# A pre-norm block (dilated local attention, then a squared-ReLU MLP) on one core: an order laid out by hand is replaced by a list scheduler, with MLP groups of four tiles, four-query attention items, and later tiles transposed by DRAM and VectorE

## Chip, cores, metric

One core of one Trainium2 chip. The metric is the device time of one execution in microseconds (us). The kernel before takes 528.69 us, the median of three runs (528.32 to 528.77).

## The reference

The input x is 2048 rows of 512 fp32 values. Both halves are residual:

```python
S, D, H, Dh, W, dil, F = 2048, 512, 32, 16, 8, 2, 1792
q, k, v = layernorm(x) @ wqkv           # 32 heads of 16
idx     = s - 2 * arange(8)             # each query sees 8 keys, two rows apart; masked below 0
o       = softmax(q . k[idx] / 4) @ v[idx]
h       = x + o @ wo
out     = h + relu(layernorm(h) @ w1 + b1) ** 2 @ w2 + b2
```

Work is in fp32 precision. TensorE multiplies fp32r operands, so each fp32 operand is split into a rounded part (names ending in h) and the rest (names ending in l), and a product is three passes: h by h, l by h, h by l.

## The kernel before

**Tiles.** The 2048 rows make 16 tiles of 128 rows. Rows are dealt so that a partition holds neighbouring queries of one parity: four tiles form a unit in which each partition has four queries (R = 4) that share a sliding window of keys, and a half-unit of two tiles (RI = 2) is called s.

**Stages.** (1) Projections: for each tile x is loaded, normalised, transposed on PE (`transposes`, L156: four 128x128 transposes into a PSUM tile `tr`), rounded by ACT (`hi`, L116) and subtracted by DVE (`lo`, L119). Then `qkv` multiplies it with the split wqkv in four pieces of 384 columns (`mm3`, L178). ACT copies the result out (L422) and SP stores it to a DRAM array `qkv_d` (L408). (2) Attention, on DVE, runs beside the projections and the MLP: an item is a half-unit by a quarter of the heads. Its windows of k and v and its q come back from `qkv_d` (L197, L210), ACT copies q to PSUM (`qp`, L217). DVE multiplies q with the eight shifted views of the window (L273) and reduces over the head's 16 values, takes a softmax, and multiplies with v (L284). Each long DVE operation has 1024 elements per partition. POOL sums over the eight keys in three halving steps (`add_up`, L343). (3) Output product: o is transposed on PE, split, and multiplied with wo (`wo_product`). DVE adds x, giving h. (4) h is normalised, transposed on PE and split, then `mlp1` and `mlp2` (L560) go over F in 14 steps of 128. A group of two tiles has 256 columns in the first product, and there are six of them; the last four tiles form one wide group of 512 columns. All of w1 and w2 is split once and stays on chip; w2 takes the space of wqkv when the projections are done.

**What sets the order.** Each engine runs its instructions in program order, and the program is written out by hand. PE's sequence is cut into slots. `at(delta, ...)` puts a chore into a later slot, `after` behind the attention of that slot, and `end_slot(pe)` adds the slot's PE time to a clock. `pump` then emits attention instructions until their estimated DVE time has caught up with that clock:

```python
while (done[until] < G) if until is not None else (now["dve"] < now["pe"]):
```

All large transfers are issued by SP, in one queue. `ready_next` places the next half-unit's loads, o transposes and output products among the steps of the current MLP group, and its h is transposed between the last three steps of that group (`h_T`).

Of the kernel before, what the change touches and what calls it, by code (L numbers as in the profile page):

```python
# [15 lines left out]
P = 128  # L16
KB = D // P
FB = F // P
R = 4
RI = 2  # L20
NS = S // P // RI
G = 8
GH = H // G
GC = GH * DH
CH = S // 2
PAD = W
EPS = 1e-5
NEG = -4.0e9
ROWS = 15
LAG = 3  # L30
SLOW = 1.1, 1.05
LAST = 2
LAGW = 2
DELAY = 3
WJ = 2
WARM = 18
# [3 lines left out]
def block_kernel(ctx, tc, x, wqkv, wo, w1, b1, w2, b2, out):  # L40
# [11 lines left out]


    CS = (CH + PAD) * GC
    qkv_d = dram.tile([2, G // 2, 3, 2, CH + PAD, GC], F32, name="qkv_d")

    def chain(e, g, c, r, ap):
        block = ((e * (G // 2) + g // 2) * 3 + c) * 2 + g % 2
        return bass.AP(tensor=qkv_d.tensor, offset=qkv_d.offset + block * CS + r * GC, ap=ap)

# [4 lines left out]

# [8 lines left out]
    wq_h = wpool.tile([P, KB, 3 * D], F32R, name="wq_h", tag="big_h")  # L74
    wq_l = wpool.tile([P, KB, 3 * D], F32R, name="wq_l", tag="big_l")
    wo_h = wpool.tile([P, KB, D], F32R, name="wo_h")
    wo_l = wpool.tile([P, KB, D], F32R, name="wo_l")
    w1_h = wpool.tile([P, KB, F], F32R, name="w1_h")
    w1_l = wpool.tile([P, KB, F], F32R, name="w1_l")
    w2_h, w2_l = {}, {}  # L80

    def row(name, shape=(P, D), dt=F32):
        return work.tile(list(shape), dt, name=name, tag="row", bufs=ROWS)

    due = {}
    late = {}
    now = {"slot": 0, "pe": 0.0, "dve": 0.0, "sub": 0}  # L90

    def at(delta, fn, *a):
        due.setdefault(now["slot"] + delta, []).append((fn, a))

    def after(delta, fn, *a):
        late.setdefault(now["slot"] + delta, []).append((fn, a))
# [8 lines left out]
    def run(chores):  # L105
        todo = chores.get(now["slot"], [])
        while todo:
            fn, a = todo.pop(0)
            fn(*a)

    def dve(t):
        now["dve"] += t


    def hi(dst, src):
        nc.scalar.copy(dst, src)  # L116

    def lo(eng, dst, src, h):
        eng.tensor_tensor(out=dst, in0=src, in1=h, op=ALU.subtract)  # L119

    stats = {}

    def norm_stats(key, src, delay=True):
        st = small.tile([P, 6], F32, name="st")
        mv = small.tile([P, 2], F32, name="mv", bufs=4)
# [13 lines left out]
        if delay:  # L139
            after(0, finish)  # L140
        else:
            finish()
# [662 lines left out]
```

## Time and profile before

| what | value |
|---|---|
| three runs | 528.69, 528.32, 528.77 us |
| profiled execution: span of its instructions | 527.5 us |
| busy share of the span: PE, PE weight load | 98%, 89% |
| DVE, ACT, POOL | 73%, 48%, 58% |
| DMA moved, all queues | 75.93 MB |
| SP's queue (q1), share of 16 engines | 75.26 MB, 47.6% |

The page gives one profiled execution, whose span lies 1.2 us below the median of the timed runs. A share of busy time is a mean over stages that differ: projections and attention run together up to about 215 us, then MLP groups and attention, and in the last 110 us almost only PE works. Instructions on PE overlap, so the time of one is read from the distance between starts.

### The profile page before, as it was taken

The numbers are of one execution on the slowest core, as the hardware profiler recorded it, in microseconds if no ns is written. First come the engines' busy times: TensorE is split into PE (matmuls) and PEld (weight loads), VectorE is DVE, ScalarE is ACT, GpSimd is POOL, SyncE is SP. The second block draws the span as 40 slices with busy tenths as digits, with TensorE's granted clock in tenths as the row PEclk, the third lists the DMA queues.
The fourth block names the chain that finished last, engine by engine and source line by source line (L and its number), as shares of the span: only waits on it lengthen the run. The fifth ranks groups of instructions, "written<-read, shape, count | busy, mean of one in ns | idle before, by whom it ended". The sixth has DMA issues, their size and how long they took to land.

```text
span 527.5 us, 8636 instructions
## 1 busy us (share of the span) xinstructions
PE 518.5 (98%) x3024; PEld 471.7 (89%) x3024; DVE 382.8 (73%) x571; ACT 252.0 (48%) x565; POOL 306.6 (58%) x421
## 2 busy tenths in 40 slices
PE   7899999999999999999999999999999999999997
PEld 6899999999999888988989898898989888888886
DVE  5559999998998799997998899699979323211113
ACT  4514554554347566545626464463536335442331
POOL 3514678788666479676877786876879717000000
PEclk8999999999999999999999999999999999999999
DMA  8578887898677453544544464454435000100002
GB/s 250 144 228 221 276 257 228 247 277 257 195 224 259 134 177 105 179 125 141 179 135 122 116 187 122 133 179 125 124 99 170 19 0 2 40 1 1 1 0 80
DMA packets 70803, 75.93 MB, mean 144 GB/s; under 512 B 6760, under 2 KB 47976, under 8 KB 70760
## 3 DMA queue, kind: packets, MB, share of 16 engines
q1 hardware_dynamic: 70616, 75.26, 47.6%
q8 instruction: 23, 0.38, 0.3%
q14 instruction: 20, 0.16, 0.1%
q10 hardware_dynamic: 144, 0.13, 0.1%
HBM read 58.50 MB, written 16.91 MB: 143 GB/s over the span
## 4 chain that ended last, share of the span: by engine, by line
PE 57%; issue 3%; POOL 3%; ACT 0%; DVE 0%; POOLq 0%; ACTq 0%
PE mm L178 25%; PE acc L560 25%; PE wo L178 5%; PE tr L156 2%; POOL rl L119 1%; POOL rs L135 1%; POOL h L497 0%; POOL pr L343 0%; PE half L581 0%; DVE pr L284 0%; POOL rs L137 0%; POOL rs L133 0%; ACT hn L151 0%; ACT r L537 0%; POOL o L343 0%
## 5 line engine op out<-in xcount | busy, mean ns | idle before, releaser
L343 POOL TENSOR_TENSOR pr<-pr 128x512 f32<-128x512 f32 (+1 forms) x128 | 131.5, 1027 | 36.8 <-DVE pr L284 31.5
L537 ACT ACTIVATE r<-mm,b_sb 128x256 f32<-128x256 f32 (+1 forms) x98 | 49.4, 505 | 120.0 <-PE mm L178 111.2
L119 POOL TENSOR_TENSOR rl<-r,rh 128x256 fp32r<-128x256 f32 x84 | 63.0, 754 | 57.6 <-ACT rh L116 57.5
L284 DVE TENSOR_TENSOR pr<-ex,v 128x1024 f32<-128x1024 f32 x64 | 78.0, 1220 | 5.5 <-POOL o L343 2.9
L273 DVE TENSOR_TENSOR pr<-qp,k 128x1024 f32<-128x1024 f32 x64 | 76.1, 1188 | 4.9 <-ACT qp L217 4.3
L178 PE MATMUL mm<-hh,w_h 128*128 128x256 f32 (+1 forms) x392 | 69.8, 300 | 0.0
L178 PE MATMUL mm<-hl,w_h 128*128 128x256 f32 (+1 forms) x392 | 69.0, 298 | 0.0
L178 PE MATMUL mm<-hh,w_l 128*128 128x256 f32 (+1 forms) x392 | 68.9, 298 | 0.0
L178 PEld LDWEIGHTS mm<-hh,w_h 128*128 128x128 f32 x392 | 59.9, 189 | 6.8 <-ACT r L537 0.2
L422 ACT COPY y<-mm 128x384 f32<-128x384 f32 x64 | 30.2, 480 | 65.3 <-PE mm L178 34.1
L560 PE MATMUL acc<-w_h,rh 128*128 128x512 f32 x192 | 58.8, 397 | 0.0
L178 PEld LDWEIGHTS mm<-hl,w_h 128*128 128x128 f32 x392 | 56.8, 191 | 2.2
L178 PEld LDWEIGHTS mm<-hh,w_l 128*128 128x128 f32 x392 | 56.7, 191 | 2.2
L560 PE MATMUL acc<-w_h,rl 128*128 128x512 f32 x192 | 57.8, 391 | 0.3 <-POOL rl L119 0.3
L560 PE MATMUL acc<-w_l,rh 128*128 128x512 f32 x192 | 57.9, 391 | 0.0
L178 PE MATMUL mm<-wq_h,xh 128*128 128x384 f32 x256 | 57.4, 344 | 0.1
L178 PE MATMUL mm<-wq_h,xl 128*128 128x384 f32 x256 | 55.6, 338 | 0.6 <-DVE xl L119 0.4
L178 PE MATMUL mm<-wq_l,xh 128*128 128x384 f32 x256 | 55.0, 335 | 0.0
L119 DVE TENSOR_TENSOR rl<-r,rh 128x512 fp32r<-128x512 f32 x14 | 9.7, 692 | 59.8 <-ACT rh L116 59.8
L178 PEld LDWEIGHTS mm<-wq_h,xl 128*128 128x128 f32 x256 | 45.9, 190 | 1.2 <-DVE xl L119 1.2
L178 PEld LDWEIGHTS mm<-wq_l,xh 128*128 128x128 f32 x256 | 45.7, 189 | 0.0
L538 ACT ACTIVATE r<-r 128x256 f32<-128x256 f32 (+1 forms) x98 | 44.0, 449 | 3.1
(84 smaller groups left out, 855.2 us busy)
## 6 DMA issues: line engine op xcount, KB each, us to landing
k<-qkv_d SPq DMA_DIRECT2D x48, 288.0 KB, 2.7
v<-qkv_d SPq DMA_DIRECT2D x48, 288.0 KB, 2.7
qkv_d<-y SPq DMA_DIRECT2D x32, 384.0 KB, 4.3
xt<-in_A_x_dram SPq DMA_DIRECT2D x16, 256.0 KB, 4.3
q<-qkv_d SPq DMA_DIRECT2D x32, 128.0 KB, 2.9
h<-in_A_x_dram SPq DMA_DIRECT2D x16, 256.0 KB, 3.8
out_dram<-h SPq DMA_DIRECT2D x15, 256.0 KB, 3.1
raw<-in_B_w_dram SPq DMA_DIRECT2D x16, 224.0 KB, 4.4
```

The source lines that it names most:

```text
L119: eng.tensor_tensor(out=dst, in0=src, in1=h, op=ALU.subtract)
L135: nc.gpsimd.tensor_tensor(out=rs[:, 0:1], in0=rs[:, 1:2], in1=mhalf, op=ALU.pow)
L156: nc.tensor.transpose(tr[:, k, :], src[:, k * P:(k + 1) * P], ident)
L178: nc.tensor.matmul(ps, l(k), r(k), start=(n == 0), stop=(n == 3 * KB - 1))
L273: nc.vector.tensor_tensor(out=pr.rearrange("p i w h d -> p i w (h d)"), in0=qp[:, j].unsqueeze(2).to_broadcast([P, RI, W, GC]), in1=kwin, ...
L284: nc.vector.tensor_tensor(out=p2, in1=vwin, op=ALU.mult, in0=e1[:, :, :, j * GH:(j + 1) * GH].unsqueeze(4).to_broadcast([P, RI, W, GH, DH]))
L343: nc.gpsimd.tensor_tensor(out=dst, in0=p2[:, :, :w], in1=p2[:, :, w:2 * w], op=ALU.add)
L422: nc.scalar.copy(y[:, :, t % RI * GC:(t % RI + 1) * GC], ps[:, :3 * GP].rearrange("p (j c) -> p j c", j=6))
L537: nc.scalar.activation(r, ps, AF.Relu, bias=b1_sb[:, f:f + 1])
L538: nc.scalar.activation(r, r, AF.Square)
L560: nc.tensor.matmul(acc[j], l[:, j * P:(j + 1) * P], w[f], start=(f == 0 and n < len(js)), stop=(f == last and n >= len(terms) - len(js)))
```

## The change

The source is rewritten; the arithmetic of the block stays the same.

- **Order.** Every piece of work becomes a task with engines that may run it, a guessed duration, and the tiles that it reads and writes. `deadlines` goes backward from PE's planned times, and `schedule` deals the tasks out, engine by engine, the one that can start first and is due first. The order that results is fixed before the program runs.
- **Transposes.** The first four x tiles and o and h of unit 0 are transposed on PE. All others (`turned`) go to DRAM in 512-byte pieces (`turn_write`), come back rearranged in 128-byte pieces (`turn_read`, 2048 a tile), and DVE transposes the 32x32 blocks (`turn`).
- **Projections.** The first four tiles as before; the other twelve in three products of 512 columns (q, k, v), stored two tiles at a time.
- **Attention.** An item is now four queries by 128 channels (a quarter of the heads); long DVE operations have 2048 elements. Logits and exponentials are in PSUM (`le`).
- **MLP.** Four groups of four tiles, all 512 columns wide. w1 has six of its 14 steps in space of its own and eight in wqkv's. w2 is split in the first group, written to DRAM (`w2_d`), and read again step by step in the other three, into four buffers (`w2s`).
- **Results.** h and the MLP results of units 0 to 2 are written to DRAM (`park_h`, `park`) and added at the end (`unpark`), together with b2.
- **Norms.** Statistics of x tiles 4 to 15 and of h of units 1 to 3 move from DVE to ACT (`norm_act`), those of the first tiles stay on DVE.

```diff
-G = 8
+Q = 32
+IQ = 2
+G = 4
+FA = 6
+BY_PE = (0,)
+TO_MLP = 10
...
+    def deadlines(self):
+        for t in reversed(self.tasks):
+            slack = SLACK[t.only] if t.only else 1.0
+            d = min([s.due for s in t.succs], default=1e6) - t.dur - t.lat - slack
+            if t.pe is not None:
+                d = t.pe
+            elif t.by is not None:
+                d = min(d, t.by)
...
+                    key = (s if s > free[eng] + 0.02 else free[eng],
+                           t.due - 1e3 if t.pe is not None and t.early else t.due, t.n)
+                    if pick is None or key < pick[0]:
+                        pick = key, t, s
+                if pick and (best is None or pick[2] < best[2]):
+                    best = eng, pick[1], pick[2]
...
-    def end_slot(pe):
-        now["pe"] += pe
-        run(due)
-        pump()
-        run(late)
-        now["slot"] += 1
...
+    def norm_act(src, dst):
+            nc.scalar.activation(sq.get(), src.get(), AF.Copy, accum_out=s[:, 0:1])
+            nc.scalar.activation(s[:, 1:2], s[:, 0:1], AF.Copy, scale=-1.0 / D)
+            nc.scalar.activation(sq.get(), src.get(), AF.Square, bias=s[:, 1:2],
+                                 accum_out=s[:, 2:3])
+            nc.scalar.activation(s[:, 3:4], s[:, 2:3], AF.Copy, scale=1.0 / D, bias=EPS)
...
+    def turn_write(d, src):
+        load(512, 512, lambda q: q.dma_start(
+            turn_ap(d, 0, [P, KB], [KB * D, Q], [D, KB], [1, P]),
+            src.get().rearrange("p (k m) -> p k m", k=KB)), r=[src], w=[("d", d)])
+    def turn_read(d, dst, n=1, r=()):
+        load(2048 * n, 128, lambda q: q.dma_start(
+            dst.get().rearrange("p (m c) -> p m c", c=Q),
+            turn_ap(d, 0, [Q, KB], [n * KB * D, Q], [P, n * KB * KB], [1, Q])),
+            r=list(r) + [("d", d)], w=[dst])
+    def turn(src, dst, part=slice(None)):
+        vec(D, lambda: nc.vector.transpose(dst.get().rearrange("p k m -> p (k m)"),
+                                           src.get()[:, part]), r=[src], w=[dst])
+    def turned(src):
+        d = Dram(dram.tile([P * D], F32, name="t_d"))
+        turn_write(d, src)
+        back, t = row("back"), row("turned", (P, KB, P))
+        turn_read(d, back)
+        turn(back, t)
+        return t
...
+    def item(u, g, due):
...
+        for n, i0 in enumerate((0, IQ)):
+            pr = buf("pr", (P, IQ, W, GC), name="pr")
+            vec(2048, lambda pr=pr, i0=i0: nc.vector.tensor_tensor(
+                out=pr.get(),
+                in0=qp.get()[:, i0:i0 + IQ].unsqueeze(2).to_broadcast([P, IQ, W, GC]),
+                in1=window(ks.get(), i0, [1, GC]), op=ALU.mult),
+                r=[qp, ks], w=[pr], by=due + 5 * n)
...
+    def w1_of(part, f):
+        if f < FA:
+            return w1a[part][:, f]
+        return big[part][:, KB + f - FA, :].rearrange("p (k c) -> p k c", k=KB)
...
+    def first_w2(f):
+        raw = row("raw2")
+        load(128, 2048, lambda q: q.dma_start(raw.get(), w2[f * P:(f + 1) * P, :]), w=[raw],
+             ahead=AHEAD)
+        t = buf("pair", (P, 2, D), F32R, "w2s")
+        hi(D, lambda: t.get()[:, 0], raw.get, r=[raw], w=[(t, 0)])
+        lo(D, lambda: t.get()[:, 1], raw.get, lambda: t.get()[:, 0], r=[raw, (t, 0)], w=[(t, 1)])
+        load(128, 4096, lambda q: q.dma_start(w2_d[f], t.get().bitcast(F32)), r=[(t, 0), (t, 1)],
+             w=[("w2d", f)], by=plan.pe + 5)
+        return t
+    def get_w2(f):
+        t = buf("pair", (P, 2, D), F32R, "w2s")
+        load(128, 4096, lambda q: q.dma_start(t.get().bitcast(F32), w2_d[f]), r=[("w2d", f)],
+             w=[(t, 0), (t, 1)], ahead=AHEAD)
+        return t
...
+    def park(t, a):
+        m = row("m")
+        plan.add({"ACT": ac(D), "DVE": dv(D)},
+                 lambda e: nc.scalar.copy(m.get(), a.get()) if e == "ACT"
+                 else nc.vector.tensor_copy(m.get(), a.get()), r=[a], w=[m], by=plan.pe)
+        load(128, 2048, lambda q: q.dma_start(m_d[t], m.get()), r=[m], w=[("md", t)],
+             by=plan.pe + 5)
+    def unpark(t, due):
+        m, h = row("m"), row("h")
+        load(128, 2048, lambda q: q.dma_start(m.get(), m_d[t]), r=[("md", t), "done"], w=[m],
+             by=due)
+        load(128, 2048, lambda q: q.dma_start(h.get(), h_d[t]), r=[("hd", t), "done"], w=[h],
+             by=due)
+        tt("DVE", D, m.get, m.get, lambda: b2_sb, ALU.add, r=["b2"], w=[m], by=due + 5)
+        tt("DVE", D, m.get, m.get, h.get, ALU.add, r=[h], w=[m], by=due + 5)
+        b, e, i = where(t)
+        load(128, 2048, lambda q: q.dma_start(out_v[b, e, i], m.get()), r=[m], by=due + 8)
...
-    def x_T(t):
-        tr = transposes(xt.pop(t))
-        xT[t] = row("xh", (P, KB, P), F32R), row("xl", (P, KB, P), F32R)
-        at(0, hi_T, tr, [xT[t][0]])
-        after(0, lo_T, tr, [xT[t][0]], [xT[t][1]])
+    def x_chain(t):
+        xt = load_x(t, ahead=AHEAD)
+        norm_act(xt, xt)
+        xT[t] = split(turned(xt), "x")
...
-    def o_T(s, j):
-        pump(until=s)
-        tr = transposes(o_t[s][:, j, :])
-        oT[s, j] = row("oh", (P, KB, P), F32R), row("ol", (P, KB, P), F32R)
-        at(0, hi_T, tr, [oT[s, j][0]])
-        after(0, lo_T, tr, [oT[s, j][0]], [oT[s, j][1]])
+        if u in BY_PE:
+            parts = {}
+            for g in range(G):
+                o = os_[u, g]
+                tr = pe_turn([lambda i=i, o=o: o.get()[:, i, :] for i in range(R)],
...
+            d = Dram(dram.tile([R * P * D], F32, name="o_d"))
+            for g in range(G):
+                o = os_[u, g]
+                load(512, 512, lambda q, g=g, o=o: q.dma_start(
+                    turn_ap(d, g * D, [P, KB], [R * KB * D, Q], [KB * D, R], [1, P]), o.get()),
+                    r=[(o, 0), (o, IQ)], w=[("d", d, g)])
+            back = buf("unit", (P, R * D), name="back")
+            turn_read(d, back, R, r=[("d", d, g) for g in range(G)])
+            for i in range(R):
+                t = row("turned", (P, KB, P))
+                turn(back, t, slice(i * D, (i + 1) * D))
+                oh, ol = split(t, "o")
+                wo_product(u * R + i, (lambda k, oh=oh: oh.get()[:, k, :], [oh]),
+                           (lambda k, ol=ol: ol.get()[:, k, :], [ol]), h[i], False,
+                           first=first + 2.73 * i)
...
-    for s in range(NS - LAST):
-        acc = [psum.tile([P, D], F32, name=f"acc{j}") for j in range(RI)]
...
+            w2s[f] = first_w2(f) if u == 0 else get_w2(f)
+            hid[f] = mlp1(f, engs)
+            if f >= 2:
+                g = f - 2
+                if last and g == FB - 1 - LAGW:
...
+            if not last and f == TO_MLP:
+                to_mlp(u + 1, need[u + 1])
+        split_h()
+        if not last:
+            for g in (FB - 2, FB - 1):
+                mlp2(g, hid[g], w2s[g], acc, range(R), False, g == FB - 1, True)
+            for j in range(R):
+                park(u * R + j, acc[j])
```

The order of instructions at three places, of before and of the change. First SP's queue while x tiles are still being fetched and the first attention runs. k, q: windows of attention; raw: weights; xt: a tile of x; y: results of the projections. Before:

```order
L197 DMA v<-qkv_d 128x704
L460 DMA raw<-in_B_w_dram 128x448
L408 DMA qkv_d<-y_90 128x6x128
L197 DMA k<-qkv_d 128x704
L210 DMA q<-qkv_d 128x2x128
```

The change at the same stage; t_d is the DRAM copy of a tile that is to be turned, back what returns:

```order
L416 DMA xt<-in_A_x_dram 128x512
L500 DMA k<-qkv_d 128x1408
L374 DMA t_d<-xt 4x128x128
L567 DMA raw<-in_B_w_dram 128x4x128
L416 DMA xt<-in_A_x_dram 128x512
L481 DMA qkv_d<-y 128x4x256
L379 DMA back<-t_d 128x16x32
```

Between the windows, weights and stores that both have, each later x tile has two more transfers, one out and one back, the second of 128-byte pieces, and the tile can be turned only when both are done.

Second, ACT at the end of the first MLP group. Before, where h of the next two tiles is rounded (hh) among the activations (r) of the old group:

```order
L217 COPY qp<-q 128x256
L116 CAST hh<-tr 128x2x128 x2
L537 ACTIVATE r<-mm,b_sb 128x256
L538 ACTIVATE r<-r 128x256
L116 CAST rh<-r 128x256
L116 CAST hh<-tr 128x2x128 x2
```

The change; m is the copy of an accumulator that is to be parked, big_h the rounded h of the next group, turned the transposed tile:

```order
L652 ACTIVATE r<-mm,b_sb 128x512
L654 ACTIVATE r<-r 128x512
L292 CAST rh<-r 128x512
L690 COPY m<-acc 128x512
L292 CAST big_h<-turned 128x4x128 x2
L690 COPY m<-acc 128x512
L292 CAST big_h<-turned 128x4x128 x2
```

The roundings of all four tiles come after the last activation of the old group, with copies of its accumulators ahead of and between them.

Third, PE at the same edge. Before, where transposes of the next h (hn) lie among the last second products (acc) of a two-tile group:

```order
L560 MATMUL acc_2646<-w_h,rl 128x512
L560 MATMUL acc_2647<-w_h,rl 128x512
L156 MATMUL tr<-ident,hn 128x128 x4
L560 MATMUL acc_2646<-w_h,rh 128x512
L560 MATMUL acc_2647<-w_h,rh 128x512
L560 MATMUL acc_2646<-w_l,rh 128x512
```

The change, last products of group 0 and first of group 1 (mm, with h in big_h and big_l):

```order
L665 MATMUL acc<-w2s,rl 128x512 x4
L665 MATMUL acc<-w2s,rh 128x512 x8
L665 MATMUL acc<-w2s,rl 128x512 x4
L401 MATMUL mm<-big_h,w1a_h 128x512 x8
L401 MATMUL mm<-big_h,w1a_l 128x512 x8
L401 MATMUL mm<-big_l,w1a_h 128x512 x8
```

PE goes from the last acc of one group straight to the first mm of the next, with no transposes and no other matmuls between.

More of the change, by code (lines that the diff above doesn't have):

```diff
@@ L105, in run @@
[L105 to L125, printed above, removed]
[L126 to L133 removed]
+    w1a_h = wpool.tile([P, FA, KB, P], F32R, name="w1a_h")
@@ new lines, in buf, with act @@
+    def buf(tag, shape, dt=F32, name=None):
+        pool = pools.get(tag, att if tag in ("kv", "q", "pr", "o") else work)
+        return Buf(tag, lambda: pool.tile(list(shape), dt, name=name or tag, tag=tag,
+                                          bufs=bufs[tag]))
+    def row(name, shape=(P, D), dt=F32):
+        return buf("row", shape, dt, name)
+    engines = {"DVE": nc.vector, "POOL": nc.gpsimd, "ACT": nc.scalar, "SP": nc.sync}
+    def act(n, fn, extra=0.0, **k):
+        return plan.add({"ACT": ac(n) + extra}, lambda e: fn(), **k)
@@ new lines, in pe_turn, with go, split @@
+    def pe_turn(srcs, r, **k):
+        tr = buf("ps", (P, KB, P), name="tr")
+        def go(e):
+            for n, s in enumerate(srcs):
+                nc.tensor.transpose(tr.get()[:, n, :], s(), ident)
+        plan.add({"PE": 0.45}, go, r=list(r) + ["ident"], w=[tr], **k)
+        return tr
+    def split(src, name, engs=("POOL", "DVE")):
+        h, l = row(name + "h", (P, KB, P), F32R), row(name + "l", (P, KB, P), F32R)
+        hi(D, h.get, src.get, r=[src], w=[h])
+        lo(D, l.get, src.get, h.get, r=[src, h], w=[l], engs=engs)
+        return h, l
@@ new lines, in mlp2, with run, go @@
+    def mlp2(f, hid, w2s, acc, js, first, last, split_):
+        rh, rl = hid
+        def run(terms, r, lead, end):
+            def go(e):
+                for n, (l, wn, j) in enumerate(terms):
+                    nc.tensor.matmul(acc[j].get(), l.get()[:, j * P:(j + 1) * P],
+                                     w2s.get()[:, wn], start=lead and n < len(js),
+                                     stop=end and n >= len(terms) - len(js))
+            plan.add({"PE": len(terms) * 0.228}, go, r=r, w=[acc[j] for j in js])
+        one = [(rh, 0, j) for j in js] + [(rh, 1, j) for j in js]
+        two = [(rl, 0, j) for j in js]
+        if split_:
+            run(one, [rh, (w2s, 0), (w2s, 1)], first, False)
+            run(two, [rl, (w2s, 0)], False, last)
+        else:
+            one.insert(1, two[0])
+            run(one, [rh, rl, (w2s, 0), (w2s, 1)], first, last)
```

1105 lines of the change are left out of this document (546 added, 559 removed).

## The prediction

> **What bounds the kernel now.** I read the page first: busy shares, then the 40 slices.
>
> ```profile
> PE 518.5 (98%) x3024; PEld 471.7 (89%) x3024; DVE 382.8 (73%) x571; ACT 252.0 (48%) x565; POOL 306.6 (58%) x421
> ...
> PEclk8999999999999999999999999999999999999999
> DMA  8578887898677453544544464454435000100002
> ```
>
> TensorE (PE) is busy in 98% of the span, at full granted clock after the first slice. VectorE (DVE) has 73%; the DMA engines are loaded in the first third and nearly idle in the last fifth. Busy time of a pipelined engine does not say what one instruction costs, so next come stages, the chain that ended last, and the timeline, where starts can be subtracted.
>
> ```profile
> 19.39:211.00 191.61, 191.16 (x1148) 184.16 (x1148) 166.40 (x248) 96.85 (x219) 125.97 (x168) 1.00 0.72 215
> 211.00:418.00 207.00, 207.00 (x1292) 186.06 (x1291) 181.50 (x265) 104.24 (x255) 158.32 (x212) 1.00 0.46 137
> 418.00:527.50 109.50, 105.98 (x518) 88.93 (x516) 21.87 (x38) 41.83 (x76) 13.25 (x20) 1.00 0.04 15
> ```
>
> (Columns: stage, length, busy PE, weight loads, DVE, ACT, POOL, clock, DMA share, GB/s.) From 19.39 us to the end PE waits for almost nothing, in three stages whose other engines differ widely. So PE's work is the time, and I price it by spacing of starts.
>
> ```profile
> 322.23 1.43 PE mm L178 x12
> 323.66 1.39 PE acc L560 x6
> 325.05 1.43 PE mm L178 x12
> ...
> 456.13 2.72 PE acc L560 x12
> 458.85 2.72 PE mm L178 x12
> ```
>
> Twelve matmuls of 256 columns take 1.43 us, six of 512 with two tiles per weight 1.39, twelve of 512 take 2.72 (in the last, wide group).
>
> ```profile
> 122.11 0.85 PE L178 MATMUL mm<-wq_h,xh 128*128 128x384 f32 x4
> 122.80 0.85 PE L178 MATMUL mm<-wq_h,xl 128*128 128x384 f32 x4
> ...
> 257.32 0.64 PE L178 MATMUL mm<-hl,w_h 128*128 128x256 f32 x4
> 257.80 0.60 PE L156 MATMUL tr<-ident,o 128*128 128x128 f32 x4
> 258.15 0.72 PE L178 MATMUL mm<-hh,w_h 128*128 128x256 f32 x4
> 258.71 0.64 PE L178 MATMUL mm<-hh,w_l 128*128 128x256 f32 x4
> ```
>
> Four matmuls of 384 columns are 0.69 apart, so 12 take 2.08. A set of four transposes takes 0.35 and makes the next four matmuls 0.08 longer (0.56 for 0.48): 0.43.
>
> The sum before: 64 projections x 2.08 = 133.1; 16 output products x 2.72 = 43.5; first MLP product 84 x 1.43 + 14 x 2.72 = 158.2; second 84 x 1.39 + 14 x 2.72 = 154.8; 48 transpose sets x 0.43 = 20.6. Together 510.3 of the span of 527.5. Of the 17.2 left, 9.4 lie ahead of the dense part: at the second row below four projections and four sets, 10.0 us, were done:
>
> ```profile
> 18.68 0.86 PE L178 MATMUL mm<-wq_l,xh 128*128 128x384 f32 x4
> 19.39 0.85 PE L178 MATMUL mm<-wq_h,xh 128*128 128x384 f32 x4
> ```
>
> **The change, part by part, on PE.** The same columns are multiplied. Projections: 16 x 2.08 + 36 x 2.72 = 131.2 (-1.9). First MLP product: all 56 wide, 152.3 (-5.9); second likewise, 152.3 (-2.5). Transposes: the first four x tiles, and o and h of the first unit, stay on PE, 12 sets of 48 (-15.5). Sum 484.5: 25.8 us less, and 501.7 if all else stayed. Everything below is what could take this back.
>
> **Vector, Scalar and GpSimd work.**
>
> ```profile
> L284 DVE TENSOR_TENSOR pr<-ex,v 128x1024 f32<-128x1024 f32 x64 | 78.0, 1220 | 5.5 <-POOL o L343 2.9
> L273 DVE TENSOR_TENSOR pr<-qp,k 128x1024 f32<-128x1024 f32 x64 | 76.1, 1188 | 4.9 <-ACT qp L217 4.3 <-POOL o L343 0.4
> L119 DVE TENSOR_TENSOR xl<-tr,xh 128x512 fp32r<-128x512 f32 x16 | 10.9, 679 | 0.1
> L343 POOL TENSOR_TENSOR pr<-pr 128x512 f32<-128x512 f32 x64 | 83.5, 1305 | 31.8 <-DVE pr L284 31.5
> L343 POOL TENSOR_TENSOR pr<-pr 128x256 f32<-128x256 f32 x64 | 48.0, 750 | 5.0
> L537 ACT ACTIVATE r<-mm,b_sb 128x512 f32<-128x512 f32 x14 | 9.6, 689 | 42.7 <-PE mm L178 42.7
> 28.80 1.22 DVE L273 TENSOR_TENSOR pr<-qp,k 128x1024 f32<-128x1024 f32 x1 [3.52 <-ACT qp L217]
> 200.00:300.00 100.00, 100.00 (x621) 89.56 (x620) 90.72 (x135) 52.28 (x129) 77.85 (x103) 1.00 0.47 139
> ```
>
> Long DVE operations grow by about 1.05 us per 1024 elements (679 ns for 512, 1188 to 1220 for 1024), so one of 2048 is about 2.27 us, and 96 of them 218 us, for 192 of about 1.2 (231). Added are 36 DVE transposes, an operation that the trace lacks: bounded by 0.35 (half a 512 subtraction) and 1.22 (the 1024 row); I take 0.69, as 512 elements in and out, 25 us. Added too: 24 sums that put parked results together, 16 us; gone are 24 pairs of statistics, which move to ScalarE (ACT) as three operations of 512 at about 0.65 and three tiny ones, 24 x 2.6 = 62 us at most on top of 252, far below the span. POOL's adds of 1024 cost 1305 + 2 x (1305 - 750) ns, 2.4 us, half as many as the 512 ones before. No engine's total nears the span; what counts is the rate up to where the attention of a unit (four tiles) must be ready. Before started its first item at 28.80 (row below), after the same four tiles; the DVE rows from there to unit 1's turning sum to some 177 us by these means (55 long ones, 125; 25 subtractions and 12 turns of 0.69, 26; some 60 small operations, sums and statistics, 26), and fall due near 210. That is 98% of 181 us by means; but busy time before (382.8) is 0.91 of the sum of its groups' times (some 422), since neighbours overlap: 89%, close to the 90.72. DVE alone just keeps up, with little to spare for waits.
>
> **DMA in the first 200 us** is the place where the change pays. In the rows of SP's queue shown with the change, each later x tile goes out (t_d) and comes back through DRAM between windows and stores; 36 tiles do in all, and the split w2 is written to DRAM once and read back in three groups. Adding shapes, SP moves 59.6 MB by its 176th transfer, the return of o for unit 1: attention's reads 17.3, stores of q, k, v 12.7, x and weights in 15.5, split w2 out 4.7, turns of x and o 8.4, h parked 1.0. Before:
>
> ```profile
> q1 hardware_dynamic: 43702, 40.25, 71.8%
> qkv_d<-y SPq DMA_DIRECT2D x31, 384.0 KB, 4.4
> 60.00:65.00 5.00, 1.00 1.06 362
> 65.00:70.00 5.00, 1.00 1.02 329
> ...
> out_dram<-h ACTq DMA_DIRECT2D x1, 128.0 KB, 1.8
> b_sb<-in_B_b_dram SPq DMA_DIRECT2D x1, 7.0 KB, 4.3
> ```
>
> (First row: 19 to 205 us of before.) 40.25 MB in 71.8% of 186 us is 301 GB/s at full share, and filled windows moved 329 to 362. The returning tiles use packets of 128 bytes, 32,768 of them up to there (12 tiles x 2048, then 8192). Below, such a packet costs its bytes at 330 GB/s over 16 engines, 6 ns; above, the 1792 four-byte packets of the bias landed in 4.3 us, 1.8 of it fixed by the smallest store: (4.3 - 1.8) x 16 / 1792 = 22 ns. I take 14, between: 29 us (13 to 45). The other 55.4 MB need 184 us at 301, 168 at 330. So 213 us (181 to 229) must pass in the 205 between about 5 us and 210; PE asks for unit 1's output product near 212, 2 to 3 later than DVE can turn. Late by 8 less 3: +5 us (0 to +20), which once lost is not won back; afterwards 24 MB until unit 2's return lie in some 91 us (14 pairs of products and four output products), 265 GB/s, and fit. If it is late, x tiles 8 to 13 are late first, then the attention that waits on DVE behind their transposes.
>
> The Trainium skill, page "DMA: Bandwidth & Descriptors", Specifications, says that below 512 bytes a DMA does read-modify-write and misses line rate. By that rule a 128-byte packet would cost what a 512-byte one does and the sum would end above 535; the trace agrees only in part, since the four-byte packets of the bias cost at most 22 ns, less than the 27 that a 512-byte one costs below. It is rival (3).
>
> **Group edges.** At the first edge shown with the change, the copies that empty the accumulators stand on ACT ahead of and between the roundings of the next group's h, whose four tiles the group's first matmul needs, and PE has no other matmul left between the last `acc` and the first `mm`; before, matmuls of the old group covered the roundings. The first copy waits for the first accumulator, 0.7 us before PE ends; then two copies and four roundings at 0.6 each (between the 631 ns and 589 ns that ACT's 512 forms take):
>
> ```profile
> L538 ACT ACTIVATE r<-r 128x512 f32<-128x512 f32 x14 | 8.8, 631 | 0.4
> L116 ACT CAST xh<-tr 128x512 fp32r<-128x512 f32 x16 | 9.4, 589 | 3.8 <-PE tr L156 3.7
> ```
>
> 3.6 - 0.7 + signals: 3.2 us. At the second edge three copies and one rounding stand so: 2.2. Before the first group two roundings follow PE's last transposes: 1.3. The third edge has matmuls left. Together +6.8 (4 to 9; the DRAM turn itself has 19 us of matmuls over it and may add to it). The Trainium skill, "TensorE: Matmul & The Clock Gate", Part 1, halves the clock after an idle window of 3.4 us. No row of before shows a later idle; by that rule two such edges would add some 1.7 us each.
>
> **Sum.** 501.7 + 0.8 (one more 256 KB load ahead of the first weights, at 301 GB/s) + 5 + 6.8 = 514.3 for the profiled execution. Its span of 527.5 stands to a median of 528.69, +1.2: 515.5, say 516.
>
> **Rivals.** (1) All is covered: packets near 6 ns, DVE ahead, edges of 4: 501.7 + 0.8 + 4 + 1.2 = 508. For it: filled windows of 362 GB/s, and before's DMA digits after 200 us, 3 to 6. Against: the 90.72 is the most that DVE held in the stages I asked for. (2) DMA keeps the lead to the last attention and DVE waits with it: the +20 end in place of 5, 515.5 + 15 = 530; halfway 523, which is still faster. The 59.6 MB are for it, the 265 GB/s after 200 us against it. (3) Slower, by one mechanism: the 128-byte packets of the returning tiles cost what 512-byte ones cost, 512 B at 18.8 B/ns (301 GB/s by 16) = 27 ns. That is 13 ns x 32,768 / 16 = 27 us more before unit 1's product: 542. It decides from 21 ns on, where 7 ns x 32,768 / 16 = 14 us eat the gain; that lies just under the bound of 22. (4) The order, fixed beforehand, slips in many small waits (POOL's sums hold the three product buffers, SP's queue waits for a store and holds what stands behind it): some 15 us in sum, 530. Against it: before had a fixed order too, and its PE waited under 1 us after the start.
>
> **Chances.** Forecast (510 to 522, around 516) 0.50; (1) 0.18; (2) 0.14; (3) 0.10; (4) 0.08. Faster by over 0.2% (under 527.6; 0.2% is about what a measurement here can tell from no change): nearly all of the first two and most of (2), 0.79; within: 0.04 from (2) and (4); slower 0.17. Range 506 to 530: outside lie (3), and the ends of (1), (2) and (4).
>
> **What would show it.** Right: PE's matmul spacing unchanged at 2.72 per 12; no transposes after the first group begins; DMA share near 1 up to 200 us; gaps of 2 to 4 us on PE at the starts of groups 1 and 2, released by ACT's roundings; the last group dense. Wrong: PE waits for x tiles or unit 1's output product adding up to over 15 us (DMA or DVE); landing of a tile's return over 8 us (packet price); DVE transposes over 1 us; PE waiting for w2 pairs, which I cost at nothing since they are loaded ahead into four buffers and the queue after 200 us has room.

## The result and the profile after

The changed kernel takes 716.5 us, the median of four runs (716.0 to 720.4), beside 528.7 for the kernel before: a ratio of 1.356, 95% interval 1.352 to 1.360. The forecast was 516. Here and below a time is the median of the executions at the faster of two speeds; only e13 had one at the slower, 559.8 us, and it is left out. The profiled execution has a span of 714.2 us, 186.7 more than before. From its page: busy times, then the 40 slices, the load of SP's queue, and the chain that ended last, by engine and by line; the last row is the chain of the kernel before.

```profile
PE 534.7 (75%) x2232; PEld 436.7 (61%) x2232; DVE 361.0 (51%) x342; ACT 274.7 (38%) x554; POOL 299.4 (42%) x253
...
PE   7977584677759999439609991964499199589997
PEclk8987796978879999859958996996699699989999
DMA  6757674755566876467358734744546573356231
...
q1 hardware_dynamic: 155724, 125.07, 57.4%
...
DMA 36%; PE 27%; issue 12%; SPq 10%; DVE 8%; POOL 4%; ACT 4%; POOLq 0%; DVEq 0%; ACTq 0%
PE mm L401 15%; DMA back<-t_d 11%; DMA back<-o_d 10%; PE wo L401 7%; DMA t_d<-hn 5%; PE acc L665 4%; POOL rl L297 2%; DMA o_d<-o 2%; DMA m<-m_d 2%; DVE pr L515 2%; DMA raw<-in_B_w_dram 2%; DMA t_d<-xt 2%; DVE le L520 2%; SPq L640 2%; SPq L379 1%
...
PE 57%; issue 3%; POOL 3%; ACT 0%; DVE 0%; POOLq 0%; ACTq 0%
```

PE, 98% busy before, is busy 75%, with holes up to the last group, and the granted clock falls in the same slices. No engine has taken over: DVE, ACT and POOL are all idler, and DMA is not full either. The chain runs through DMA for 36%, where before it had none: 21% are returns of turned tiles (`back`), 9% the writes ahead of them (`t_d`, `o_d`). What PE waited for (us in total, times, longest):

```profile
PE mm L401 <- ACT xh L292: 52.5, 11, 11.5
PE mm L401 <- ACT big_h L292: 47.2, 4, 22.2
PE wo L401 <- ACT oh L292: 34.2, 2, 19.7
PE wo L401 <- ACT r L652: 16.0, 1, 16.0
PE acc L665 <- ACT rh L292: 10.1, 2, 8.6
```

The first four rows, 150 us, are waits for roundings of what came back through DRAM: x tiles (xh), h at the group edges (big_h), o (oh, and the 16.0, where ACT is named but o of unit 3 was under way). In the fifth, the wait of 8.6 is for a rounding that stood on ACT behind one of h whose tile had not come back. With the small ones PE waited 176 us. After a long wait matmuls go at half speed for a while: the first eight below start 3.58 us ahead of the next, eight dense ones 1.81 (517.24 to 519.05).

```profile
373.88 3.78 PE L401 MATMUL mm<-big_h,w1a_h 128*128 128x512 f32 x8 [22.22 <-ACT big_h L292]
377.46 1.05 PE L401 MATMUL mm<-big_h,w1a_l 128*128 128x512 f32 x2
...
517.24 1.98 PE L401 MATMUL mm<-big_h,w1a_h 128*128 128x512 f32 x8
519.05 1.07 PE L401 MATMUL mm<-big_h,w1a_l 128*128 128x512 f32 x4
```

So the 714.2 are the forecast 484.5 of PE's work, 176 of waits, 41 of slow clock, and some 13 of start and end beside waits. The 41 come from the trace: the granted clock stands at half in 16 stretches in which PE works (one of them at the start; before had only that one), with 81 us of busy PE in them, and half of those are lost. Where DMA stood while PE waited is seen on SP's queue, and in a window (length, granted clock, DMA share, GB/s):

```profile
76.98 0.55 SPq L379 DMA_DIRECT2D back<-t_d  x1
77.63 5.58 SPq L500 DMA_DIRECT2D k<-qkv_d  x1
...
542.32 0.56 SPq L379 DMA_DIRECT2D back<-o_d  x1
543.04 22.30 SPq L704 DMA_DIRECT2D out_dram<-m  x1
```

```profile
549.00:564.00 15.00, 0.79 0.35 54
```

The transfer behind a returning tile is held for 5.6 us, behind a unit's o for 22.3, and while it is held the DMA engines are a third busy and move 54 GB/s. The return is slow, and not because DMA is full.

### The profile page after: what moved, and what is told of

Same layout as the page of the kernel before. It is cut to its first block, busy times and chain, and to the rows that moved or that the text cites. A ratio compares the mean times of both kernels' runs of the same rounds, so it can differ in the third digit from the quotient of the medians.

```text
span 714.2 us, 6711 instructions
## 1 busy us (share of the span) xinstructions
PE 534.7 (75%) x2232; PEld 436.7 (61%) x2232; DVE 361.0 (51%) x342; ACT 274.7 (38%) x554; POOL 299.4 (42%) x253
## 4 chain that ended last, share of the span: by engine, by line
DMA 36%; PE 27%; issue 12%; SPq 10%; DVE 8%; POOL 4%; ACT 4%; POOLq 0%; DVEq 0%; ACTq 0%
PE mm L401 15%; DMA back<-t_d 11%; DMA back<-o_d 10%; PE wo L401 7%; DMA t_d<-hn 5%; PE acc L665 4%; POOL rl L297 2%; DMA o_d<-o 2%; DMA m<-m_d 2%; DVE pr L515 2%; DMA raw<-in_B_w_dram 2%; DMA t_d<-xt 2%; DVE le L520 2%; SPq L640 2%; SPq L379 1%
## 5 line engine op out<-in xcount | busy, mean ns | idle before, releaser
L553 POOL TENSOR_TENSOR pr<-pr 128x1024 f32<-128x1024 f32 (+1 forms) x64 | 121.3, 1916 | 16.1 <-DVE pr L544 16.0
L665 PE MATMUL acc<-w2s,rh 128*128 128x512 f32 x444 | 113.2, 395 | 10.1 <-ACT rh L292 10.1
L297 POOL TENSOR_TENSOR rl<-r,rh 128x512 fp32r<-128x512 f32 x45 | 59.4, 1322 | 144.0 <-ACT rh L292 128.2
L401 PE MATMUL mm<-big_h,xh 128*128 128x512 f32 (+1 forms) x208 | 63.0, 448 | 60.3 <-ACT xh L292 52.5
L665 PEld LDWEIGHTS acc<-w2s,rh 128*128 128x128 f32 x444 | 85.0, 192 | 28.9 <-ACT rh L292 10.9
L515 DVE TENSOR_TENSOR pr<-qp,k 128x2048 f32<-128x2048 f32 x32 | 72.9, 2283 | 19.6 <-POOL o L553 4.2
L520 DVE TENSOR_REDUCE le<-pr 128x128 f32<-128x2048 f32 x32 | 72.9, 2278 | 5.1 <-ACT le L533 4.5
L544 DVE TENSOR_TENSOR pr<-le,v 128x2048 f32<-128x2048 f32 x32 | 72.1, 2283 | 0.5
L665 PE MATMUL acc<-w2s,rl 128*128 128x512 f32 x222 | 62.1, 398 | 0.6 <-POOL rl L297 0.6
L401 PE MATMUL mm<-big_l,xh 128*128 128x512 f32 (+1 forms) x208 | 55.7, 413 | 0.0
```

The lines of the kernel that those rows point to most:

```text
L297: lambda e: engines[e].tensor_tensor(out=dst(), in0=src(), in1=h(), op=ALU.subtract), r=r, w=w, **k)
L401: nc.tensor.matmul(ps(), l(), rr(), start=start and i == 0, stop=stop and i == len(terms) - 1)
L515: vec(2048, lambda pr=pr, i0=i0: nc.vector.tensor_tensor(out=pr.get(), in0=qp.get()[:, i0:i0 + IQ].unsqueeze(2).to_broadcast([P, IQ, W, GC ...
L520: vec(2048, lambda pr=pr, i0=i0: nc.vector.tensor_reduce(out=lg()[:, i0:i0 + IQ].rearrange("p i w h -> p (i w h)"), in_=pr.get().rearrange ...
L544: last = vec(2048, lambda p2=p2, i0=i0: nc.vector.tensor_tensor(out=p2.get(), in1=window(vs.get(), i0, [DH, GH], [1, DH]), op=ALU.mult, in ...
L553: nc.gpsimd.tensor_tensor(out=dst, in0=p[:, :, :w], in1=p[:, :, w:2 * w], op=ALU.add)
```

## The experiments

An edit that changes tasks or their guessed durations also changes the order that the planner deals out. Only e1, e2 and e7 keep the order of the change on every engine that computes.

### Smaller packet count, another queue, no turn, and data alone (e1 to e4)

e1, 512-byte pieces in the return:

```diff
-            dst.get().rearrange("p (m c) -> p m c", c=Q),
-            turn_ap(d, 0, [Q, KB], [n * KB * D, Q], [P, n * KB * KB], [1, Q])),
+            dst.get().rearrange("p (m c) -> p m c", c=P),
+            turn_ap(d, 0, [P, P], [P * P, n * KB], [1, P])),
```

> The change as it is, with one edit: the tiles that come back from DRAM come in pieces of 512 bytes instead of 128, so 512 packets a tile instead of 2048, the same bytes, the same order on every engine. (The pieces then land in another arrangement, so the turned tiles are not the transposes: this part of the computation is changed.) Theory A, the number of small packets: behind each returning transfer SP's next transfer waits 5 to 9 us (22 behind the 8192 packets of a unit's o), about 2.7 ns a packet, and everything in SP's queue waits too. Then a tile's return should take under 3 us, that of o about 6, most of PE's 176 us of waits go, with them the slowed clock, and the time falls to 530 to 590. Rival B, the order fixed by guesses, or the length of the way through DRAM whatever the packets: PE's waits stay, the time stays over 650.

Measured: 562.6 us (ratio 1.064, 1.061 to 1.067), in the range of theory A. The return was most of the loss, 154 of the 188 us; but the edit changed the length of the pieces and the first number of the pattern (each pair of the pattern is a step and a number of entries: 4 in `[Q, KB]`, 128 in `[P, P]`) together, which showed only later.

e2, the return issued by ACT: `nc.scalar.dma_start` in place of `q.dma_start` in `turn_read`.

> The change as it is, with one edit: the same returning transfers of 128-byte packets are issued by ACT instead of SP, at the place in the order where SP had them. If theory A holds with the limit in one queue, SP's other transfers no longer stand behind the returns, while the returns take what they took (5 to 9 and 22 us), and ACT, which now waits for the write of each tile, adds waits of its own: 600 to 680. If the limit lies behind the queues (DMA engines or DRAM, theory C), SP's transfers are as late as before and ACT is held up besides: 700 or more.

Measured: 734.6 us (1.389, 1.385 to 1.393). By the range this spoke for theory C, and the trace says otherwise: beside a return that began at 424 us SP's transfers flowed, 360 GB/s in all, and when there were none the return alone went at 52 (length, granted clock, DMA share, GB/s).

```profile
425.00:428.00 3.00, 1.00 0.99 360
...
440.00:444.00 4.00, 0.50 0.35 52
```

```profile
424.13 0.54 ACTq L379 DMA_DIRECT2D back<-o_d  x1
...
483.88 11.35 ACTq L379 DMA_DIRECT2D back<-t_d  x1
```

So the limit goes with the transfer and not with its queue. SP's queue flowed beside the return, ACT was held up in its stead (11.35 us behind the returns ahead), and PE's waits came to 192 us, for 176 in the change.

e3, all tiles turned on PE, with a limit on how far PE's plan may run ahead and four more row buffers:

```diff
-BY_PE = (0,)
+BY_PE = (0, 1, 2, 3)
-ROWS = 22
+ROWS = 26
...
-        xT[t] = split(turned(xt), "x")
+        tr = pe_turn([lambda k=k: xt.get()[:, k * P:(k + 1) * P] for k in range(KB)], [xt],
+                     first=plan.pe - 8)
+        xT[t] = split(tr, "x", ("DVE",))
...
+        def parts(ht=None if pe else ht):
+            if pe:
+                ht = pe_turn([lambda k=k: hn.get()[:, k * P:(k + 1) * P] for k in range(KB)], [hn])
...
-                    if eng not in t.eng:
+                    if eng not in t.eng or (eng == "PE" and t.due > pe_due + WIN):
```

> The change with all tiles transposed on PE as in the kernel before (x 4 to 15, o and h of units 1 to 3; no turn through DRAM), the list scheduler, the four groups, the four-query items and the parked results kept; PE's planner may not run over 12 us ahead of its own plan, and four more row buffers stand where the returned o stood. PE has 36 sets of transposes more, 15.5 us. Theory A (the turn through DRAM is the whole loss): PE's work is 500, with start, edges and the late DMA of the prediction 525 to 545, clock near 1. Rival B (the order fixed by guesses, the parked results, or w2 read again cost much by themselves): 580 or more.

Measured: 547.9 us (1.035, 1.034 to 1.037), 3 above the expected range. Taking the turn through DRAM out is worth 169 of the 188 us, though PE has 15.5 us more to do; the limit on the plan is in this number too. What keeps e3 above the kernel before is another cause, taken up below.

e4, data alone:

> A kernel that only moves data (nothing of the block is computed): 1 MB from DRAM to SBUF in pieces of 128, 256, 512, 1024 and 2048 bytes, one after the other on SP's queue; 128 and 512 on ACT's; 128 on both queues at once; a plain 256 KB load behind a 128-byte transfer on the same queue; then 1 MB to DRAM in pieces of 2048, 512 and 128. Theory A: 2.7 ns a packet on one queue whatever its size up to some 800 bytes: 22 us for 128, 11 for 256, 5.6 for 512, then 3.0 (350 GB/s); the load behind waits the 22 us; both queues at once each take their 22 (the limit in the queue). Theory C (DMA engines or DRAM): both at once take 44, and 128-byte packets cost as much as 512-byte ones by bytes moved.

This run does not decide anything: the pieces of neighbouring partitions lay side by side in DRAM and most were joined (25,504 packets in all, 8,480 of them under 512 bytes), and the transfers ran in another order than written.

### Small writes, and data alone again (e5, e6)

e5 writes a tile in 128-byte pieces, already rearranged, and reads it back in long ones:

```diff
-            turn_ap(d, 0, [P, KB], [KB * D, Q], [D, KB], [1, P]),
-            src.get().rearrange("p (k m) -> p k m", k=KB)), r=[src], w=[("d", d)])
+            turn_ap(d, 0, [P, P], [Q, KB], [Q * D, KB], [1, Q]),
+            src.get().rearrange("p (k a r) -> p k a r", k=KB, r=Q)), r=[src], w=[("d", d)])
...
-            turn_ap(d, 0, [Q, KB], [n * KB * D, Q], [P, n * KB * KB], [1, Q])),
+            turn_ap(d, 0, [D, P], [P * D, n], [1, D])),
```

> The change with the small pieces moved to the other side of the turn: a tile is written to DRAM in 128-byte pieces, already rearranged (2048 packets), and comes back in 2048-byte pieces (128 packets); rows are dealt so that the roundings put the tokens in order. The result is the reference's. The run with 512-byte returns took 562.6 and left the rearranging out; this one keeps it. Theory A2 (what is slow is reading small pieces: a return of 8192 moves 55 GB/s with the DMA engines a third busy, while 8192 small writes went in some 7.6 us in the run that only moves data): returns under 3 us for a tile and under 6 for a unit, writes of a tile 2 to 3 us, time 550 to 600. Rival A1 (every 128-byte packet costs 2.7 ns of its queue, read or written): the waits only move from the return to the write, 650 or more.

> Data movement alone again, in a fixed order and with pieces that cannot be merged (in the first such run the pieces of neighbouring partitions lay side by side in DRAM and went as 512-byte packets, in an order of the scheduler's): 1 MB into SBUF on SP in pieces of 128, 256, 512, 1024 and 2048 bytes, then 128 and 512 on ACT's queue, 128 on both queues at once, 128 on SP with a plain 256 KB load behind it and another on ACT's queue, then 1 MB to DRAM in pieces of 2048, 512, 256 and 128. Nothing of the block is computed. Theory A2: 128-byte reads take 22 us (2.7 ns a packet) and 256-byte reads 11, both queues at once still about 22 each, the plain load waits 20 us behind them on SP and none on ACT's queue; writes of 128 bytes take 8 us. Theory A1: the same for reads, and 22 us for the writes. Theory C (a limit shared by all queues): both at once take 44.

e5: 560.8 us (1.060, 1.058 to 1.062), as A2 has it. e6 refutes A2 all the same. Its chain shows 8192 small reads on SP in 6.67 us, and two such transfers at once in 11.47; its list of issues has a 256 KB load that lands after 8.2 us behind small reads on the same queue, where A2 had 20, and after 3.6 on the other.

```profile
0.73 6.67 DMA t<-in_A_x_dram
...
42.73 11.47 DMA tb<-in_A_x_dram
```

```profile
t<-in_A_x_dram ACTq DMA_DIRECT2D x1, 256.0 KB, 3.6
t<-in_A_x_dram SPq DMA_DIRECT2D x1, 256.0 KB, 8.2
```

Small reads are not slow as such: the same number of 128-byte packets took 22 us in the kernel and 6.7 here. What differed was the pattern. The change's return begins, on the DRAM side, with a dimension of 4 (`[Q, KB]`); here, in e1 and in e5 it began with 128.

### The first dimension (e7, e8)

```diff
+        def four(q):
+            for a in range(KB):
+                q.dma_start(dst.get()[a * Q:(a + 1) * Q].rearrange("p (m c) -> p m c", c=Q),
+                            turn_ap(d, a * Q, [n * KB * D, Q], [P, n * KB * KB], [1, Q]))
+        load(2048 * n, 128, four, r=list(r) + [("d", d)], w=[dst])
```

> The change with one edit: each returning transfer is cut into four, one for each 32 partitions. Pieces (128 bytes, 2048 a tile), DRAM addresses, order and queue stay. In the change the pattern on the DRAM side begins with a dimension of 4 (the four blocks of 32 columns), now with one of 32. Theory E (the transfer runs on as many DMA engines as its pattern's first dimension has entries, here 4 of 16): in the change's return of 8192 packets the DMA share was 0.3 and 55 GB/s; the move-only run took 6.7 us for the same number of 128-byte packets with a first dimension of 128. So a tile's return falls to about 3 us, a unit's to 7, and the time to 555 to 585, as with 512-byte returns and with small writes (562.6, 560.8), both of which had changed the first dimension too. Theory A2 (reading small pieces in this arrangement is slow in itself): nothing changes but three more issues, 700 or more.

> Data movement alone: 1 MB from DRAM to SBUF in 128-byte pieces (8192 packets), one after the other, with a first dimension of 4, 8, 16, 32 and 128; then 4 with the pieces side by side, as the change has them; then in 512-byte pieces with 4 and 128; then 1 MB to DRAM in 512-byte pieces with 4 and 128. Nothing of the block is computed. Theory E, from 6.7 us with 128 (about 1.8 fixed, 9.5 ns a packet and engine): 4: 21; 8: 12; 16, 32 and 128: 7; side by side 21; 512 bytes: 12 to 18 with 4, 6 with 128, and so for the writes. Theory A2 (the arrangement in DRAM, not the first dimension): all with a step of 256 bytes alike, about 7, and only the one side by side slow.

e8 settles it: its first five transfers move the same pieces and differ only in this number, on the DRAM side. Windows inside its transfers, in order: 128-byte reads with a first dimension of 4, 8, 16, 32, 128, then 4 side by side; 512-byte reads with 4 and 128; 512-byte writes with 4 (length, clock, DMA share, GB/s; the share is the time of the packets over that of 16 engines, so above 1 packets of one engine overlap):

```profile
5.00:20.00 15.00, 1.00 0.35 54
26.00:33.00 7.00, 1.00 0.70 107
38.00:41.00 3.00, 1.00 1.45 202
46.00:49.00 3.00, 1.00 1.38 218
53.00:56.00 3.00, 1.00 1.38 218
62.00:77.00 15.00, 1.00 0.35 54
82.00:97.00 15.00, 1.00 0.30 57
102.00:105.00 3.00, 1.00 1.06 296
110.00:121.00 11.00, 1.00 0.27 76
```

The rate doubles from 4 to 8 and nearly so to 16, and then about stands: 54, 107, 202, 218, 218. That is what 4, 8 and 16 engines would do at 218 / 16 = 13.6 GB/s each, or 9.4 ns for a 128-byte packet. The 54 GB/s and 0.35 of the kernel's return are the first row, a quarter of the rate and share with 128. Long pieces are confined as well: 512-byte reads and writes with 4 go at 57 and 76, where reads with 128 go at 296. The Trainium skill, "DMA: Bandwidth & Descriptors", section "Why a DMA increments its semaphore by 16 and not by 1", says so: the number of engines is the largest up to 16 that divides the slowest dimension of both patterns. The trace agrees for 4, 8, 16, 32 and 128 on the DRAM side; no run here tried a number that is not a power of two.

e7: 608.2 us (1.148, 1.147 to 1.150), above its range of 555 to 585, far below 700. With the same pieces, DRAM addresses and order, 108 of the 188 us go with the first dimension of the return alone. What keeps e7 46 us above e1 stays open. It is not the writes: their pattern begins with 4 too, in the change, e1 and e7 alike. e7 has 81 more issues on SP and four times the packets of e1. The issues of returns in e7, then in e1 (shortest, median and longest ns):

```profile
L381 SPq DMA_DIRECT2D back<-t_d x96: 539/625/2880, 39.5 to 514.7; - x96
...
L379 SPq DMA_DIRECT2D back<-t_d x24: 359/376/2858, 41.5 to 469.5; - x24
```

Summed over the traces, and with those of o, they take 93 us of SP's queue in e7 and 15 in e1. That fits the difference, but no run separates issues from packets.

### What is left (e9 to e14)

e9 is e3 with the weights' subtractions on POOL alone:

```diff
-    def split_raw(dst, src_ap, shape, keys, engs=("POOL", "DVE"), count=128, packet=2048,
+    def split_raw(dst, src_ap, shape, keys, engs=("POOL",), count=128, packet=2048,
```

The same in `first_w2`. e10 is e5 with the x tiles turned on PE.

> The run with all tiles turned on PE (547.9) with one edit: the subtractions that split weights (wo, w1, w2) may be run by POOL alone instead of POOL or DVE. There PE lost some 20 us between 175 and 250 us, waiting for DVE (ol, h), which was busy 97% of 180 to 220 us, with some ten subtractions of weights in it. Theory F (DVE is the limit there, and the planner's choice of DVE for them costs PE its time): 535 to 543. Rival (the order, or attention alone fills DVE): 545 to 552.

> Small writes, long returns (as in the run of 560.8) for o and h of units 1 to 3, and the x tiles transposed on PE: 12 sets of transposes more than the change, 24 fewer than with all on PE. PE's work is 490. In the run of 560.8 PE lost some 25 us to x tiles before 125 us, when DMA was busy 0.9 of the time. If theory E is all that the turn through DRAM costs and the x tiles' share of DMA is what is left early on, the time is 525 to 542; if o and h on their way through DRAM are late by themselves, 545 to 560. Kernel before: 528.7.

e9: 541.9 us (1.023, 1.021 to 1.024), so theory F holds for 6 us. e10: 545.4 (1.030, 1.028 to 1.031), above the first range and at the foot of the second: o on its way through DRAM is late by itself (10.9 us of PE's waits). In e9 one large hole is left. PE, then DVE (start, length, and the idle time ahead):

```profile
214.16 1.98 PE L406 MATMUL wo<-wo_h,ol 128*128 128x512 f32 x8
...
218.69 1.07 PE L671 MATMUL acc<-w2s,rl 128*128 128x512 f32 x4
231.19 3.78 PE L406 MATMUL mm<-big_h 128*128 128x512 f32 x8 [11.43 <-DVE h L307]
```

```profile
212.53 4.48 DVE L549 TENSOR_TENSOR pr<-le,v 128x2048 f32<-128x2048 f32 x2
...
224.82 2.24 DVE L525 TENSOR_REDUCE le<-pr 128x128 f32<-128x2048 f32 x1
227.91 2.28 DVE L549 TENSOR_TENSOR pr<-le,v 128x2048 f32<-128x2048 f32 x1
230.44 1.37 DVE L307 TENSOR_TENSOR h<-wo,h 128x512 f32<-128x512 f32 x2 [0.26 <-issue]
```

PE had finished two output products (`wo`) at 216. The sums that empty their PSUM tiles stand on DVE behind 14 us of attention. In `deadlines` a sum's due time comes from what reads its result, which is late, and not from PE, which needs the tiles back. e11 gives them one, in e9's kernel; e12 is e10 with weights on POOL and this, e13 is e5 with both, e14 is e5 with the due time alone.

```diff
-        tt("DVE", D, h.get, ps.get, h.get, ALU.add, r=[ps], w=[h])
+        tt("DVE", D, h.get, ps.get, h.get, ALU.add, r=[ps], w=[h], by=k["first"] + 3.0)
```

> The run with all tiles turned on PE and weights split by POOL alone (541.9) with one edit: the sum of output product and x (h) gets a due time, 3 us after its product's place in the plan. There these sums stood behind 14 us of attention on DVE, and PE waited 11.4 us for the PSUM tiles that they empty, lost some 5 us more shortly before, and went on at half clock. Theory G (the missing due time is the cause of that hole): 518 to 528, so no slower than the kernel before (529). Rival H (DVE has too much to do up to there, and another attention operation is late in its place): 534 to 542.

> The run with x on PE and o and h by DRAM in small writes (545.4) with two edits: weights split by POOL alone and the due time for h. PE's work is 490, ten less than with all on PE. Theory G: 512 to 526. Rival H: 534 or more; or o's way through DRAM (PE waited 10.9 us for its rounding, in three places) stays: 526 to 534.

> The change with the small pieces on the write side (560.8), weights split by POOL alone, and the due time for h: all later tiles go through DRAM as the change means it, PE's work is 484.5. Theory G with the x tiles still late up to 125 us (25 us of waits and slow clock there): 538 to 550. If the x tiles were late only because DVE took other work first: 515 to 530.

> As the run before this one without the POOL edit: small writes and the due time for h alone. Theory G: 540 to 552, some 3 to 6 above the run with weights on POOL if DVE's load counts here as it did with all on PE (547.9 against 541.9).

e11: 525.5 us (524.2 to 526.3), a ratio of 0.992 (0.990 to 0.994), 0.8% below the kernel before. Its page, and the largest of PE's waits:

```profile
PE 511.0 (98%) x2376; PEld 426.9 (82%) x2376; DVE 340.9 (65%) x322; ACT 273.7 (52%) x553; POOL 277.0 (53%) x238
```

```profile
PE tr L363 <- DVE xt L330: 3.3, 2, 2.0
```

The hole is gone, the clock is 1.000, and theory G holds with the turn on PE. With the turn in DRAM it changes less: e12 544.0 (1.027, 1.025 to 1.029), e13 552.8 (1.042, 1.039 to 1.045), e14 554.5 (1.047, 1.044 to 1.049). e13 and e14 are above their ranges, e12 above that of theory G and inside that of rival H. There the wait moves: in e12 PE waits 1.5 us for o and 5.6 more ahead of output products, for 10.9 in e10, and 12.9 for h at the edges, for 3.3. The longest of these ends with a return, and not with attention on DVE as H has it (DVE, then PE):

```profile
269.97 0.71 DVE L396 STREAM_TRANSPOSE turned<-back 128x512 f32<-128x512 f32 x1 [3.34 <-DMA back<-t_d]
...
271.86 3.62 PE L412 MATMUL mm<-big_h,w1a_h 128*128 128x512 f32 x8 [8.43 <-ACT big_h L292]
```

e13 waits 16.4 for x tiles and 13.8 for h; beside e14, POOL's edit is worth some 2 us, within the spread of the runs, where with all on PE it was worth 6. One stage of e5 and of e11 side by side (stage, then busy PE, weight loads, DVE, ACT, POOL, clock, DMA share, GB/s):

```profile
60.00:125.00 65.00, 50.75 (x204) 39.55 (x204) 54.17 (x51) 43.51 (x95) 44.59 (x34) 0.89 0.98 272
```

```profile
60.00:125.00 65.00, 65.00 (x311) 53.78 (x310) 60.41 (x55) 48.60 (x113) 47.35 (x40) 1.00 0.81 268
```

With the x tiles through DRAM the DMA engines are full (0.98) and PE idles 14 of 65 us; without them 0.81 is enough. e10, which is e5 with the x tiles on PE, has PE busy 64.7 of these 65 us at a share of 0.75.

| run | what differs from the change | us |
|---|---|---|
| change | | 716.5 |
| e1 | returns in 512-byte pieces, first dimension 128 | 562.6 |
| e2 | returns issued by ACT | 734.6 |
| e3 | all tiles turned on PE | 547.9 |
| e5 | writes in 128-byte pieces, returns long, first dimension 128 | 560.8 |
| e7 | each return cut into four, first dimension 32 | 608.2 |
| e9 | e3, weights split by POOL | 541.9 |
| e10 | e5, x tiles on PE | 545.4 |
| e11 | e9, due time for h | 525.5 |
| e12 | e10, weights split by POOL, due time for h | 544.0 |
| e13 | e5, weights split by POOL, due time for h | 552.8 |
| e14 | e5, due time for h | 554.5 |

## Why the prediction was wrong, point by point

- **PE's work and DVE's main prices were right.** Twelve matmuls of 512 columns take 2.72 (eight in 1.81). e11 has 36 sets of transposes more than the change, 15.5 us: 484.5 + 15.5, with the 17.2 left over before and the 0.8 of the sum, are 518.0, and its span is 523.2. DVE's long operations were put at 2.27, its transposes at 0.69 us:

```profile
L385 DVE STREAM_TRANSPOSE turned<-back 128x512 f32<-128x512 f32 x36 | 24.8, 702 | 193.3 <-DMA back<-t_d 141.8
...
L515 DVE TENSOR_TENSOR pr<-qp,k 128x2048 f32<-128x2048 f32 x32 | 72.9, 2283 | 19.6 <-POOL o L553 4.2
```

- **The step that failed is the paragraph on DMA, "32,768 of them" shared by 16 engines.** The price of a packet, taken as 14 ns and bounded by 6 and 22, measured 9.4. The divisor was wrong: the returns run at the rate of four engines, and 32,768 x 9.4 / 4 is 77 us where the sum had 29. All 27 returns, 24 of 2048 packets (4.8 us) and 3 of 8192 (19.3), come by this price to 173 us of SP's queue. The writes are confined too: at e8's 76 GB/s the 256 KB of one take 3.4 us, an estimate. Both numbers stood in view: the 4 of the return is the `KB` in `turn_read`'s `[Q, KB]`, that of the write stands in the row `t_d<-xt 4x128x128`. The prediction took bytes and packets from them and not that number. The page of the Trainium skill that it cited, "DMA: Bandwidth & Descriptors", has the rule in another section than the one it weighed.
- **The second step that failed: transfers were summed as a volume, and they are a chain.** With 77 for 29 the sum would still end at some 564. SP's queue is in order, so a held return delays windows, stores and weights behind it (5.6 and 22.3 us in the rows above), and the round trip itself lies between one piece of PE's work and the next. That "the DRAM turn itself has 19 us of matmuls over it" did not cover it: the edges waited 22.2, 18.1 and 6.1 us, beside 0.8 ahead of the first group, whose h is turned on PE. In e5, with fast returns, the first edge waited 6.8, where the order of copies and roundings on ACT was priced at 3.2 (some 2 us of it, an estimate, are e5's four longer roundings, 1.13 us for 0.62); with h turned on PE (e11) no wait at an edge is over 1.
- **The clock** was priced for two edges; the trace has 15 slow stretches after the start, 38 us in all. The eight matmuls shown above took 1.8 us more than dense ones; the mean of a stretch is 2.5. From the Trainium skill's rule ("TensorE: Matmul & The Clock Gate", Part 1: half clock after an idle window of 3.4 us) the prediction had estimated 1.7.
- **Rival (3)** had the sign and not the cause: packets of 128 bytes stay under the 21 ns from which it would decide, and 542 was too low since it, too, divided by 16. **Rival (2)**, DMA in the lead, was hidden behind this. e5, e13 and e14 show the first part of it: a share of 0.96 to 0.99 from 60 to 125 us, 0.85 or less later, at 553 to 561 where it was priced at 530. So the change as it was meant, with its transfers spread, is still slower than before.
- **Rival (1)**, all covered, fell with the rate of the returns; its 6 ns a packet was too low as well. **Rival (4)**, the order, was priced at 15 us in many small waits. With the turn on PE it is of that size, in the plan of e3: e3 to e11 is 22 us, 6 by where weights are split and 16 by one due time. It was one stretch in which PE waited for DVE more than many small waits.
- **"DVE alone just keeps up"** had no term of its own in the sum. In e9 DVE is busy 37.8 of the 40 us from 180 to 220 and what PE needs stands behind other work; its order counts for more than its load.
- **At nothing, rightly:** w2 read again in each group. e11 does it, and no wait of PE there names w2.

## What to carry to other kernels

Read the first dimension of each transfer's pattern, on both sides, before its bytes: with 4 and 8 on the DRAM side it set the rate here (54 and 107 GB/s, for 218). Price a way through DRAM as a chain on its queue (write, signal, return, and what stands ahead of both), not as volume, and ask which matmuls cover each link. In a scheduler with due times, an operation that empties a PSUM tile needs the due time of whoever wants that tile next: this was worth 16 us here.

## What the runs showed of the hardware that was not expected

- 128-byte reads are cheap: 9.4 ns a packet on each of 16 engines, 218 GB/s, beside 296 in 512-byte pieces. A first dimension of 4 takes 1 MB from some 5 us to 19 by these rates (54 GB/s), and in pieces of 512 bytes from 3.5 to 18 (57).
- A return at 54 GB/s leaves room to the other queue (360 GB/s in all in e2), but holds back its own (22.3 us in the change).
- ACT's rounding takes 1.10 us where e5 makes it read its tile in another order than it lies, for 0.62 in the change (row of e5: shortest, median and longest ns, first and last start; row of the change: busy us, mean ns, idle time before):

```profile
L292 ACT CAST xh<-turned x10: 1067/1104/1155, 44.8 to 126.7; 128x512 fp32r<-128x512 f32 x10
...
L292 ACT CAST xh<-turned 128x512 fp32r<-128x512 f32 x12 | 7.4, 617 | 48.7 <-DVE turned L385 42.8 <-issue 5.9
```
